# Key-value sums of a linear-attention kernel on four column strips of TensorE, and one spread on four row strips

## The chip, the core and the metric

The kernel runs on one core of one Trainium2 chip. The core has a matrix engine (TensorE, PE in the profile, with its weight loads shown apart as PEld), three engines for elementwise work (VectorE or DVE, ScalarE or ACT, GpSimd or POOL) and SyncE (SP), which here only issues DMAs. Each engine works through its own instructions in order; semaphores tie them together. TensorE reads SBUF and writes PSUM, which has eight banks of 128 partitions by 512 fp32 numbers.

The metric is the time of one execution on the device, in microseconds. The kernel before takes 426.39 us, the median of three runs (424.61 to 426.71).

## The reference

Two blocks, A and B, are applied in turn, twice, with the same weights; each is added to its input. The input has 2048 rows of 512 numbers.

```python
def _A_ref(x, wqkv, w_phi, wo):
    B, S, D = x.shape
    H = 32; Dh = D // H
    qkv = (x @ wqkv).reshape(B, S, 3, H, Dh).transpose(2, 0, 3, 1, 4)
    q, k, v = qkv[0], qkv[1], qkv[2]
    pq = jnp.einsum("bhsd,hdf->bhsf", q, w_phi)
    pk = jnp.einsum("bhsd,hdf->bhsf", k, w_phi)
    phi_q = jnp.concatenate([_softmax(pq, axis=-1), _softmax(-pq, axis=-1)], axis=-1)
    phi_k = jnp.concatenate([_softmax(pk, axis=-1), _softmax(-pk, axis=-1)], axis=-1)
    kv = jnp.einsum("bhsf,bhsd->bhfd", phi_k, v)
    z  = jnp.einsum("bhsf->bhf", phi_k)
    num = jnp.einsum("bhqf,bhfd->bhqd", phi_q, kv)
    den = jnp.einsum("bhqf,bhf->bhq", phi_q, z)[..., None] + 1e-6
    o = num / den
    return o.transpose(0, 2, 1, 3).reshape(B, S, D) @ wo

def _B_ref(x, W_gate, W_up, W_down):
    gate = jnp.einsum("bsd,df->bsf", x, W_gate)
    up = jnp.einsum("bsd,df->bsf", x, W_up)
    gate = gate * (gate > 0).astype(gate.dtype)
    return jnp.einsum("bsf,fd->bsd", gate * up, W_down)

x = x + _A_ref(_layernorm(x), A_wqkv, A_w_phi, A_wo)
x = x + _B_ref(_layernorm(x), B_W_gate, B_W_up, B_W_down)
x = x + _A_ref(_layernorm(x), A_wqkv, A_w_phi, A_wo)
x = x + _B_ref(_layernorm(x), B_W_gate, B_W_up, B_W_down)
```

Block A is linear attention with 32 heads of 16 numbers. For each head, keys and queries go through a 16 by 16 map and two softmaxes of 16 features each (one of the values, one of their negatives; called the two signs below). `kv` is then a 32 by 16 matrix for each head, summed over all 2048 rows, and `z` the sum of the key features.

## The kernel before

The 2048 rows are 16 tiles of 128 rows, and four tiles are a slab (`st` 0 to 3). The activations stay in SBUF (`x_sb`). At the start the map `w_phi` is folded into the key and query weights (`fold`, L400), so that keys come out of one product.

For each slab, `into_a` normalizes and transposes the rows and calls `keys` (L470). `keys` makes, tile by tile, the key logits and the values on PE, two exponentials on ACT (`expk`, one for each sign), the softmax sums and their reciprocals on DVE (`Zk`, `rZk`), a copy of the values on ACT (`vsb`, with a seventeenth column of ones for each head), and on POOL two products of values and reciprocals (`vhat`, one for each sign, L498). Then come the key-value sums of the slab (L501 to L515). The features are cut into eight groups `g`: two signs (`sg`) by four chunks (`c`) of 128 features, which are eight heads. For each group, four products, one for each tile, accumulate 128 features by 136 columns (eight heads by seventeen). Each is a product of every head with every head in the group; only the diagonal blocks are wanted. Three, three and two groups share a PSUM bank, and each bank is added into `kvsum` on DVE (L511, L514).

When all four slabs are summed, `sums` (L517) cuts the diagonal blocks out with `mask8`, a 128 by 8 mask that says which head a feature belongs to: eight operations write the weights `ZDw` of the denominators and eight the weights `kvbd` of the numerators.

`out_of_a` then goes slab by slab. `queries` (L533) makes the query features `expq`. `attend` (L542) multiplies them with `ZDw` on PE for the denominators (small products of 16 columns, 32 for each slab), works out on ACT and DVE one factor for each row, head and sign (`atok`), and transposes these factors into `aT`. Each factor must be spread over the sixteen features of its head. For slab 0 this is done on PE, with eight products with `EC`, a matrix of zeros and ones (L584); four of the eight results are multiplied into `expq` by DVE straight out of PSUM (L586), and four are first copied to SBUF by ACT (L590) and then multiplied (L591). `VIA` (L426) says which. For the other slabs SP writes `aT` to a scratch in HBM (L575), and eight DMAs read it back with each row sixteen times (L577). The numerators are 32 products on 32 by 32 places of the array (L600), whose outputs go to four banks. They are divided from the outset, so that a copy to `oT` and the product with `wo` follow. `glu` (L626) is block B; it has most of the products.

The order of the instructions on each engine is made by a planner (`schedule`, L119): each operation carries an estimate of how long it occupies its engine (`occ`) and when its result is there (`lat`). The planner takes the operation that can start first and breaks ties by program order. It also hands out the eight PSUM banks; an operation that needs several new banks waits until that many have been released. `plan` (L191) turns the dependences into semaphore waits. Every changed operation or estimate so changes the order of all engines.

The parts that the change touches:

Of the kernel before, what the change touches and what calls it, by code (L numbers as in the profile page):

```python
# [12 lines left out]
P = 128  # L13
# [233 lines left out]
def build_kernel(nc, A_x, A_wqkv, A_w_phi, A_wo, W_gate, W_up, W_down, out):  # L247
# [8 lines left out]
    with ExitStack() as ctx:  # L256
# [26 lines left out]
        kvsum = sb("kvsum", [8, 136], FP32)  # L283
        kvbd = sb("kvbd", [2, NC, 128])
# [16 lines left out]
        EC = sb("EC", [8, 128])  # L301
        ident = sb("ident", [128])
        mask8a = sb("mask8a", [8])
        mask8 = sb("mask8", [8])
        abT = sb("abT", [8, 512])
        scratch = [nc.dram_tensor(f"spread{i}", (64, 512), BF16, kind="Internal").ap() for i in range(2)]
# [72 lines left out]
        for i in range(NWARM):  # L379
# [8 lines left out]
        op("act", lambda e: e.activation(EC[:].rearrange("p g (h j) -> p (g h) j", j=16), ident[:, 0:64].unsqueeze(2).to_broadcast([P, 64, 16]), ACT.Copy),  # L388
           reads=[R("ident"), R("tables")], writes=[R("EC")], occ=1000, name="EC")

        op("dve", lambda e: e.tensor_tensor(BD.rearrange("p c (h f) -> p c h f", f=16),
# [34 lines left out]
        VIA = lambda c, sg: sg == 1  # L426
# [43 lines left out]
        def keys(st, b):  # L470
# [30 lines left out]
            for g0, g1 in ((0, 3), (3, 6), (6, 8)):  # L501
                ps = bank(f"kv{st}{g0}")
                for g in range(g0, g1):
                    sg, c = g // 4, g % 4
                    for j, i in enumerate(tiles):
                        mm(ps, (lambda o: lambda p: p.f32()[:, o:o + 136])((g - g0) * 136), expk[:, i, sg, c * 128:(c + 1) * 128],
                           vhat[:, i, sg, c * 8:(c + 1) * 8, :], j == 0, j == 3, [R("ek", i, sg), R("vh", i, sg)], 136, f"kv{st}")
                n = (g1 - g0) * 136
                dst = kvsum[:, g0:g1, :].rearrange("p g n -> p (g n)")
                if st == 0:  # L510
                    op("dve", (lambda ps, dst, n: lambda e: e.tensor_copy(dst, ps.f32()[:, 0:n]))(ps, dst, n),  # L511
                       reads=[ps], writes=[R("kvs", g0)], occ=490, lat=580, name="kvs")
                else:
                    op("dve", (lambda ps, dst, n: lambda e: e.tensor_tensor(dst, dst, ps.f32()[:, 0:n], ALU.add))(ps, dst, n),  # L514
                       reads=[ps, R("kvs", g0)], writes=[R("kvs", g0)], occ=490, lat=580, name="kvs")  # L515

        def sums():  # L517

            kvv = kvsum[:].rearrange("p g (h e) -> p g h e", e=17)
            for g0, g1 in ((0, 3), (3, 6), (6, 8)):  # L520
                for g in range(g0, g1):
                    sg, c = g // 4, g % 4
                    op("dve", (lambda g, sg, c: lambda e: e.scalar_tensor_tensor(ZDw[:, sg, c, 8:16], kvv[:, g, :, 16], float(EPS_DEN) if sg == 0 else 0.0,
                                                                               mask8[:], ALU.add, ALU.mult))(g, sg, c),
                       reads=[R("kvs", g0), R("mask8")], writes=[R("ZDw", sg, c)], occ=77, lat=160, name="zdw")
            for g0, g1 in ((0, 3), (3, 6), (6, 8)):
                for g in range(g0, g1):
                    sg, c = g // 4, g % 4
                    op("dve", (lambda g, sg, c: lambda e: e.tensor_tensor(kvbd[:, sg, c, :].rearrange("p (h d) -> p h d", d=16), kvv[:, g, :, 0:16],
                                                                        mask8[:].unsqueeze(2).to_broadcast([P, 8, 16]), ALU.mult))(g, sg, c),  # L530
                       reads=[R("kvs", g0), R("mask8")], writes=[R("kvbd", sg, c)], occ=201, lat=290, name="kvbd")
# [214 lines left out]
```

## Time and profile before

| | us |
|---|---|
| median of three runs | 426.39 |
| profiled execution | 424.71 |
| its span, first to last instruction | 423.0 |
| PE busy | 402.1 |
| DVE busy | 275.3 |
| ACT busy | 213.6 |
| POOL busy | 69.3 |
| key-value products (256), busy | 24.4 |
| `vhat` on POOL (64 of 1105 ns) | 68.5 |
| numerator products on 32 by 32 places (256), busy | 5.6 |
| spread products of slab 0 (16), busy | 4.2 |

The profiled execution is 1.7 us below the median. Busy time of PE is the union of matmuls that overlap: a 512-column matmul lasts 379 ns, while the next one starts 216 ns after it. The mean granted clock of PE is 0.988 of full speed; it is lower only in two stretches, around 85 to 95 and 270 to 290 us.

The run has these stages: weights and the folding (to 11.6 us), the first layer's norms, keys and key-value sums (to 69 us), attention of the first slabs of layer 0 (to 91 us), block B of layer 0 mixed with attention of later slabs and the keys of layer 1 (to 269 us), and the same for layer 1, without keys behind it (to the end).

### The profile page before, as it was taken

To read this page: it belongs to the slowest core of one execution; us is meant where nothing else is said; L and a number is where in the kernel's file an instruction comes from. 1 tells how busy PE (TensorE), PEld (TensorE's weight loads), DVE (VectorE), ACT (ScalarE), POOL (GpSimd) and SP (SyncE) were. 2 spreads that over 40 slices of the span, in tenths; PEclk is the share of its full clock that TensorE was granted. 3 is DMA by queue.
4 is the path that set the end of the run, shared out by engine and by line. 5 is a ranking of instruction groups with operands and counts; after the bars stand their busy time and mean duration, and the time that the engine had idled before them with its cause. 6 is when DMAs were issued, how large, how long until landed. Compare 5 with 4: busy or idle time off the path is not lost.

```text
span 423.0 us, 6858 instructions
## 1 busy us (share of the span) xinstructions
PE 402.1 (95%) x2684; PEld 205.1 (48%) x2731; DVE 275.3 (65%) x587; ACT 213.6 (50%) x432; POOL 69.3 (16%) x71
## 2 busy tenths in 40 slices
PE   7999999599999999999999999977999999999997
PEld 4555555354444545455455445533444544444443
DVE  4999768968479647767774446876932842664332
ACT  5999897655246522834183169855522430342320
POOL 0258780000007000620052008000000000000000
PEclk9999999989999999999999999969999999999999
DMA  8960000330000000200000000022101001301001
GB/s 265 326 210 2 2 0 7 102 107 0 2 0 2 0 2 10 97 0 2 0 2 0 2 2 2 8 99 70 39 1 50 2 0 50 108 2 37 14 0 50
DMA packets 16800, 17.66 MB, mean 42 GB/s; under 512 B 1568, under 2 KB 15744, under 8 KB 16768
## 3 DMA queue, kind: packets, MB, share of 16 engines
q1 hardware_dynamic: 15552, 16.62, 12.0%
q10 hardware_dynamic: 1216, 0.61, 0.5%
q8 instruction: 21, 0.34, 0.3%
q14 instruction: 11, 0.09, 0.1%
HBM read 14.73 MB, written 2.49 MB: 41 GB/s over the span
## 4 chain that ended last, share of the span: by engine, by line
PE 76%; ACT 15%; DVE 6%; DMA 1%; issue 1%; ACTq 0%; DVEq 0%
PE pb L323 72%; ACT expq L539 4%; ACT expk L487 3%; PE pb L327 3%; ACT ytile L449 2%; ACT vsb L495 2%; DMA hT<-in_A_wqkv_dram 1%; DVE expq L591 1%; ACT yT L463 1%; DVE stats L435 1%; PE pb L600 1%; DVE expq L586 1%; DVE Zk L489 1%; ACT Wqp L420 0%; ACT abT L590 0%
## 5 line engine op out<-in xcount | busy, mean ns | idle before, releaser
L639 ACT ACTIVATE gate_sb<-pb 128x512 bf16<-128x512 f32 (+1 forms) x88 | 52.8, 600 | 130.3 <-PE pb L323 130.2
L498 POOL TENSOR_TENSOR vhat<-vsb,rZk 128x544 bf16<-128x544 bf16 x64 | 68.5, 1105 | 193.5 <-DVE rZk L491 187.1
L641 DVE TENSOR_TENSOR hT<-gate_sb,pb 128x512 bf16<-128x512 bf16 (+1 forms) x88 | 59.6, 683 | 52.6 <-PE pb L323 52.3
L323 PE MATMUL pb<-yT,Wu 128*128 128x512 bf16 (+1 forms) x345 | 91.1, 379 | 0.2
L323 PE MATMUL pb<-yT,Wg 128*128 128x512 bf16 (+1 forms) x341 | 90.6, 379 | 0.6
L323 PE MATMUL pb<-Wd,hT 128*128 128x512 bf16 (+3 forms) x355 | 76.8, 372 | 0.4
L624 DVE TENSOR_TENSOR x_sb<-x_sb,pb 128x512 bf16<-128x512 bf16 x55 | 36.4, 685 | 48.6 <-PE pb L323 48.6
L323 PEld LDWEIGHTS pb<-Wd,hT 128*128 128x128 bf16 (+1 forms) x363 | 35.4, 98 | 40.1
L323 PEld LDWEIGHTS pb<-yT,Wu 128*128 128x128 bf16 (+1 forms) x352 | 34.9, 100 | 38.4 <-issue 0.4
L323 PEld LDWEIGHTS pb<-yT,Wg 128*128 128x128 bf16 (+1 forms) x352 | 34.4, 100 | 38.1 <-issue 1.4
L435 DVE BATCH_NORM_STATS2 stats<-x_sb 128x6 f32<-128x512 bf16 x64 | 42.4, 680 | 2.2 <-ACT x_sb L619 1.4
L489 DVE TENSOR_REDUCE Zk<-expk 128x64 f32<-128x1024 bf16 x32 | 38.4, 1204 | 7.7 <-ACT expk L487 7.5
L539 ACT ACTIVATE expq<-pb 128x512 bf16<-128x512 f32 x64 | 35.0, 696 | 12.9 <-PE pb L323 12.9
L487 ACT ACTIVATE expk<-pb 128x512 bf16<-128x512 f32 x64 | 36.3, 639 | 2.3 <-PE pb L323 0.7
L323 PE MATMUL pb<-wo_sb,oT 128*128 128x512 bf16 x121 | 31.9, 399 | 2.2 <-DVE oT L608 1.7
L323 PE MATMUL pb<-wv,yT 128*128 128x512 bf16 x124 | 33.1, 379 | 0.3
L323 PE MATMUL pb<-Wkp,yT 128*128 128x512 bf16 x124 | 32.2, 379 | 0.4 <-DVE yT L460 0.2
L323 PE MATMUL pb<-yT,Wqp 128*128 128x512 bf16 x122 | 30.9, 379 | 0.4 <-ACT Wqp L420 0.2
L463 ACT ACTIVATE yT<-pb 128x512 bf16<-128x512 bf16 x52 | 27.2, 608 | 6.3 <-PE pb L327 6.2
L610 ACT ACTIVATE oT<-pb 128x512 bf16<-128x512 f32 x28 | 15.1, 609 | 24.4 <-PE pb L600 23.6
L591 DVE TENSOR_TENSOR expq<-expq,abT 128x512 bf16<-128x512 bf16 x56 | 21.9, 424 | 8.1 <-DMA abT<-spread 8.1
L323 PE MATMUL pb<-vhat,expk 128*128 128x136 bf16 x256 | 24.4, 223 | 0.2
(68 smaller groups left out, 327.4 us busy)
## 6 DMA issues: line engine op xcount, KB each, us to landing
abT<-spread SPq DMA_DIRECT2D x48, 128.0 KB
out_dram<-x_sb SPq DMA_DIRECT2D x15, 128.0 KB, 1.7
x_sb<-in_A_x_dram SPq DMA_DIRECT2D x3, 512.0 KB, 8.8
Wg<-in_B_W_gate_dram SPq DMA_DIRECT2D x1, 1376.0 KB
Wu<-in_B_W_up_dram SPq DMA_DIRECT2D x1, 1376.0 KB
Wd<-in_B_W_down_dram SPq DMA_DIRECT2D x1, 1280.0 KB
hT<-in_A_wqkv_dram ACTq DMA_DIRECT2D x2, 256.0 KB, 5.8
wv<-in_A_wqkv_dram SPq DMA_DIRECT2D x1, 512.0 KB, 5.8
```

The costliest lines, as they stand in the source:

```text
L323: op("pe", lambda e: e.matmul(view(ps), lhsT, rhs, start=start, stop=stop), reads=reads, writes=[ps], occ=max(25.0, 0.4167 * n + 2.6), lat ...
L435: op("dve", (lambda t: lambda e: e.bn_stats(stats[:, t, :], x_sb[:, t, :]))(t), reads=[R("x", t)], writes=[R("st", t)], occ=580, lat=680, ...
L463: op("act", (lambda ps, dst: lambda e: e.activation(dst, b16half(ps).rearrange("p (c n) -> p c n", c=NC), ACT.Copy))(ps, dst), reads=[ps], ...
L487: op("act", (lambda i, s, pk: lambda e: e.activation(expk[:, i, s, :], full(pk), ACT.Exp, scale=1.0 - 2.0 * s))(i, s, pk), reads=[pk], wri ...
L489: op("dve", (lambda i, zb: lambda e: e.tensor_reduce(Zk[:, zb, :], expk[:, i, :, :].rearrange("p s (h f) -> p (s h) f", f=16), AX.X, ALU.a ...
L498: op("pool", (lambda i, s, vb, rz: lambda e: e.tensor_tensor(vhat[:, i, s, :, :], vsb[:, vb, :, :], rZk[:, rz, s * 32:(s + 1) * 32].unsque ...
L539: op("act", (lambda c, s, ps: lambda e: e.activation(expq[:, st, c, s, :], full(ps), ACT.Exp, scale=1.0 - 2.0 * s))(c, s, ps), reads=[ps], ...
L591: op("dve", (lambda c, sg, gi: lambda e: e.tensor_tensor(expq[:, st, c, sg, :], expq[:, st, c, sg, :], abT[:, gi, :], ALU.mult))(c, sg, gi ...
L610: op("act", (lambda i, pn: lambda e: e.activation(oT[:, g, i, :], full(pn), ACT.Copy))(i, pn), reads=[pn], writes=[R("oT", g, i)], occ=480 ...
L624: op("dve", lambda e: e.tensor_tensor(x_sb[:, t, :], x_sb[:, t, :], full(ps), ALU.add), reads=[R("x", t), ps], writes=[R("x", t)], occ=597 ...
L639: op("act", (lambda m, gb, pg: lambda e: e.activation(gate_sb[0:m, gb, :], pg.f32()[0:m, :], ACT.Relu))(m, gb, pg), reads=[pg], writes=[R( ...
L641: op("dve", (lambda m, gb, hb, pu: lambda e: e.tensor_tensor(hT[0:m, hb, :], gate_sb[0:m, gb, :], pu.f32()[0:m, :], ALU.mult))(m, gb, hb, pu),
```

## The change

Four things change.

First, the key-value products are made for two heads at a time. A group of 128 features is cut into four strips of 32 features (two heads), and each strip is multiplied only with the 34 columns of its own two heads. The four strips lie side by side on the array's columns (`tile_position=(0, 32 * i)`), and their results on 32 partitions each. A slab has 8 groups by 4 strips by 4 tiles, 128 products with a weight load each, where it had 32. They are two operations of the planner, one for each two tiles, each with `occ` 500. All groups together need 272 columns, so one bank holds a slab's sums, and one operation of DVE evacuates them (`occ` 350). `kvsum` shrinks from 8 by 136 to 8 by 34 columns.

Second, `sums` needs three operations of DVE in place of sixteen: the small constant is added to `z`, all of `ZDw` is written at once, and all of `kvbd` at once. `kvbd` now has 32 columns for each group. A new mask `mask2` says which of the two heads of a strip a feature belongs to.

Third, the spread of slab 0 is made by two operations of four products, each on a row strip of 32 rows (`tile_position=(32 * c, 0)`), one operation for each sign. Each takes four banks at once. `EC` shrinks from 8 to 2 groups of 128 columns and is made from a small reduction `E16` on DVE. `VIA` now takes the chunks 1 and 3 of both signs, in place of sign 1 of all chunks: four of eight, as before.

Fourth, for the row strips the rows of `aT` are laid out so that each chunk has 32 rows of which 16 are used. The write-out to the scratch has 128 rows in place of 64 (131072 bytes in place of 65536); the reads are as large as before.

```diff
@@ set-up
-        op("act", lambda e: e.activation(EC[:].rearrange("p g (h j) -> p (g h) j", j=16), ident[:, 0:64].unsqueeze(2).to_broadcast([P, 64, 16]), ACT.Copy),
-           reads=[R("ident"), R("tables")], writes=[R("EC")], occ=1000, name="EC")
+        op("dve", lambda e: e.tensor_reduce(E16[:], ident[:].rearrange("p (c r) -> p r c", r=32)[:, 0:16, :], AX.X, ALU.add),
+           reads=[R("ident")], writes=[R("E16")], occ=200, name="E16")
+        op("act", lambda e: e.activation(EC[:].rearrange("p s (h j) -> p (s h) j", j=16), E16[:].unsqueeze(2).to_broadcast([P, 16, 16]), ACT.Copy),
+           reads=[R("E16"), R("tables")], writes=[R("EC")], occ=400, name="EC")
+        op("dve", lambda e: e.tensor_reduce(mask2[:], mask8[:].rearrange("p (i h) -> p h i", h=2), AX.X, ALU.add),
+           reads=[R("mask8")], writes=[R("mask2")], occ=100, name="mask2")
...
-        VIA = lambda c, sg: sg == 1
+        VIA = lambda c, sg: c % 2 == 1
@@ keys
-            for g0, g1 in ((0, 3), (3, 6), (6, 8)):
-                ps = bank(f"kv{st}{g0}")
-                for g in range(g0, g1):
-                    sg, c = g // 4, g % 4
-                    for j, i in enumerate(tiles):
-                        mm(ps, (lambda o: lambda p: p.f32()[:, o:o + 136])((g - g0) * 136), expk[:, i, sg, c * 128:(c + 1) * 128],
-                           vhat[:, i, sg, c * 8:(c + 1) * 8, :], j == 0, j == 3, [R("ek", i, sg), R("vh", i, sg)], 136, f"kv{st}")
...
+            ps = bank(f"kv{st}")
+            def products(js):
+                def fn(e):
+                    for j in js:
+                        for g in range(8):
+                            sg, c = g // 4, g % 4
+                            for i in range(4):
+                                f0 = c * 128 + 32 * i
+                                ins = e.matmul(ps.f32()[32 * i:32 * i + 32, g * 34:g * 34 + 34], expk[:, tiles[j], sg, f0:f0 + 32],
+                                               vhat[:, tiles[j], sg, 8 * c + 2 * i:8 * c + 2 * i + 2, :], start=j == 0 and g == 0, stop=j == 3,
+                                               skip_group_check=True, tile_position=(0, 32 * i))
+                    return ins
+                return fn
+            for js in ((0, 1), (2, 3)):
+                op("pe", products(js), reads=[R("ek", tiles[j], sg) for j in js for sg in range(2)] + [R("vh", tiles[j], sg) for j in js for sg in range(2)],
+                   writes=[ps], occ=500, lat=700, name=f"kv{st}")
+            flat = kvsum[:].rearrange("p g n -> p (g n)")
+            if st == 0:
+                op("dve", lambda e: e.tensor_copy(flat, ps.f32()[:, 0:272]), reads=[ps], writes=[R("kvs")], occ=350, lat=440, name="kvs")
+            else:
+                op("dve", lambda e: e.tensor_tensor(flat, flat, ps.f32()[:, 0:272], ALU.add), reads=[ps, R("kvs")], writes=[R("kvs")], occ=350, lat=440, name="kvs")
@@ sums
+            op("dve", lambda e: e.tensor_scalar(kvv[:, 0:4, :, 16], kvv[:, 0:4, :, 16], float(EPS_DEN), None, op0=ALU.add),
+               reads=[R("kvs")], writes=[R("kvs")], occ=70, lat=160, name="eps z")
+            op("dve", lambda e: e.tensor_tensor(ZDw[:].rearrange("p s c n -> p (s c) n")[:, :, 8:16].rearrange("p g (i h) -> p g i h", h=2),
+                                                kvv[:, :, :, 16].unsqueeze(2).to_broadcast([P, 8, 4, 2]),
+                                                mask8[:].rearrange("p (i h) -> p i h", h=2).unsqueeze(1).to_broadcast([P, 8, 4, 2]), ALU.mult),
+               reads=[R("kvs"), R("mask8")], writes=[R("ZDw")], occ=140, lat=230, name="zdw")
+            op("dve", lambda e: e.tensor_tensor(kvbd[:].rearrange("p s c (h d) -> p (s c) h d", d=16), kvv[:, :, :, 0:16],
+                                                mask2[:].unsqueeze(1).unsqueeze(3).to_broadcast([P, 8, 2, 16]), ALU.mult),
+               reads=[R("kvs"), R("mask2")], writes=[R("kvbd")], occ=340, lat=430, name="kvbd")
@@ attend
-                dma("sp", lambda e: e.dma_start(scr, aT[0:64, g, :]), reads=[R("aT", g)], writes=[rs], nbytes=65536, name=f"aTo{st}")
+                dma("sp", lambda e: e.dma_start(scr, aT[:, g, :]), reads=[R("aT", g)], writes=[rs], nbytes=131072, name=f"aTo{st}")
...
-                        mm(ps, full, EC[:, gi, :], aT[:, g, :], True, True, [R("EC"), R("aT", g)], 512, f"ab{st}")
...
+        def spread(g, sg):
+            pss = [bank(f"ab0{c}{sg}") for c in range(NC)]
+            def products(e):
+                for c in range(NC):
+                    r = slice(32 * c, 32 * c + 32)
+                    ins = e.matmul(full(pss[c]), EC[r, sg, :], aT[r, g, :], start=True, stop=True, tile_position=(32 * c, 0))
+                return ins
+            op("pe", products, reads=[R("EC"), R("aT", g)], writes=pss, occ=450, lat=650, name="ab0")
+            for c in range(NC):
+                scale_by(0, c, sg, pss[c])
```

`scale_by`, which is not shown, holds the multiplications of L585 to L592, unchanged but for `VIA`.

## The prediction

> **What bounds the kernel now.** I read the page's shares and slices first, then the chain that ended last, then busy time by stretch, then the timeline around the two kinds of product that the change touches.
>
> ```profile
> PE 402.1 (95%) x2684; PEld 205.1 (48%) x2731; DVE 275.3 (65%) x587; ACT 213.6 (50%) x432; POOL 69.3 (16%) x71
> PE 76%; ACT 15%; DVE 6%; DMA 1%; issue 1%; ACTq 0%; DVEq 0%
> ```
>
> ```profile
> 11.60:49.50 37.90, 35.89 (x273) 20.05 (x275) 36.45 (x75) 37.28 (x79) 23.43 (x22) 1.00 0.45 141
> 49.50:69.00 19.50, 19.27 (x213) 12.14 (x217) 13.82 (x37) 14.81 (x30) 10.75 (x11) 1.00 0.01 2
> 69.00:91.00 22.00, 16.77 (x173) 8.90 (x173) 16.61 (x50) 16.31 (x37) 0.00 (x0) 0.92 0.22 72
> 91.00:247.00 156.00, 155.05 (x907) 77.16 (x924) 106.30 (x200) 63.79 (x124) 25.75 (x24) 1.00 0.04 12
> 247.00:269.00 22.00, 21.89 (x220) 12.84 (x222) 13.28 (x36) 20.65 (x44) 8.53 (x8) 1.00 0.01 1
> ```
>
> The columns of the second fence are stretch, length, then busy PE, weight loads, DVE, ACT, POOL, granted clock, DMA share and GB/s. From 49.5 to 69 and from 91 to 269 us TensorE has nearly no idle time and heads the chain: a microsecond of PE work there is a microsecond of the end. From 11.6 to 49.5 us the chain runs through ACT (37.28 of 37.90 busy), with DVE and PE close behind. From 69 to 91 (and, alike, 269 to 291) slab 0 of a layer passes the attention alone, and DVE and ACT set the pace. The eight key-value sums lie at 20, 35, 46, 58 us (layer 0) and 133, 176, 219, 258 us (layer 1): five or six of eight where PE is the bound.
>
> The rows that price the change:
>
> ```profile
> 137.84 0.93 PE L323 MATMUL pb<-vhat,expk 128*128 128x136 bf16 x13
> 65.76 2.42 PE L323 MATMUL pb<-ZDw,expq 128*128 128x16 bf16 x90
> 119.54 1.68 PE L323 MATMUL pb<-Wd,hT 128*128 128x512 bf16 x7
> 121.14 0.65 PE L600 MATMUL pb<-expq,kvbd 32*32 32x512 bf16 x32
> 121.73 0.82 PE L323 MATMUL pb<-yT,Wg 128*128 128x512 bf16 x3
> ...
> 84.90 0.20 PEld L600 LDWEIGHTS pb<-expq,kvbd 32*32 32x32 bf16 x32 [2.45 <-DVE expq L591]
> 76.50 0.33 PEld L600 LDWEIGHTS pb<-expq,kvbd 32*32 32x32 bf16 x32
> 76.64 0.19 PEld L600 LDWEIGHTS pb<-expq,kvbd 32*32 32x32 bf16 x4
> ```
>
> The second number is the group's time from first start to last end. The reader is to see four prices. A 136-column product takes (0.93 - 0.22)/12 = 59 ns from start to start (0.22 is one matmul's own duration). A 16-column product on the whole array takes (2.42 - 0.17)/89 = 25 ns. Products on separate 32x32 places start far closer: after a wait of 2.45 us all 32 weight loads start within 0.20 - 0.09 = 0.11 us, 3.5 ns apart. But at 76.50, right behind a quick run of 18 small products, the same 32 loads need 0.33, and the last four (the third row, cut out of the second) start (0.19 - 0.09)/3 = 34 ns apart. I read this as supply: up to about 32 load-and-matmul pairs stand ready in front of PE, and when they are used up a new pair comes every 34 ns.
>
> **The change, part by part.**
>
> *Key-value sums on PE.* Removed: 32 products of 136 columns per slab, 16 per two tiles: 16 x 59 ns = 0.95 us. Added: 64 products of 34 columns with a weight load each per two tiles, as one operation. The trace has no such product. From below: 64 x 3.5 ns = 0.22 us (places never used twice in a row). From above: 64 x 34 ns = 2.18 us (nothing ready, all supplied). I take 32 pairs ready, because PE comes from 512-column products (216 ns for each pair, so supply runs ahead), and 32 supplied: 32 x 34 = 1.09 us, if a strip itself can go on every 4 x 17 = 68 ns, which the 25 ns of the small products leaves room for. Then the change of the array's division: the last 512-column product before the L600 group starts at 119.54 + 1.68 - 0.38 = 120.84, L600 at 121.14, 0.30 later where 0.22 is usual; behind it the last start is 121.14 + 0.65 - 0.37 = 121.42 and the next matmul 121.73, 0.31 later. So some 0.09 us at each end, 0.18 per operation. Sum per two tiles: 1.09 + 0.18 - 0.95 = +0.32 us; bounds -0.55 and +1.41. Sixteen such: +5.1 us, bounds -8.8 and +22.6.
>
> How much counts: the twelve operations of slabs 2 to 7 in full, 3.8 us; the four of slabs 0 and 1 lie where ACT heads the chain and PE has 2 us idle in 37.9: none to all of 1.3 us, half taken, 0.6. Together +4.4.
>
> The operation also waits for both tiles' vhat on POOL (1.1 us for each half tile) where single products slipped in before. Behind it on PE stand the gate and up products or the queries, and behind those ACT's gate and DVE's h, which idle 130 and 53 us over the run. It cannot start before the last vhat, but neither could the last 10 of the old ones. I take 0; a stall of one vhat, 1.1 us, in a slab or two is the upper end.
>
> The Trainium skill bears on this price: "TensorEngine Tiling (Array Packing)", Instruction Overhead, says that a matmul pays some 60 cycles however few columns it has, and warns against taking the tiling factor from a dimension that is already small. The Trainium skill, "TensorE: Matmul & The Clock Gate", Back-to-back issue gap, puts those 60 cycles at about 25 ns for up to 64 columns; by it an operation would be an estimated 64 x 25 ns = 1.6 us instead of 1.09. The trace agrees for the whole array (25 ns) and not for separate places (3.5 ns).
>
> *DVE.* Three evacuations per slab, 0.58 + 0.58 + 0.43 us, become one of 272 columns, 0.43 (its row is there already): -1.15 us, eight times. The sums before each layer, 8 x 0.163 + 8 x 0.291 = 3.6 us, become three operations: 0.16 for the bias, 0.16 to 0.29 for 64 elements (0.23 taken), 0.43 for 256 elements by the 272-column row; 0.8 in all. DVE loses 15 us of work, of which I credit nothing: in the PE-bound stretches it idles anyway, and between 21 and 32 us, where DVE is full, ACT is as full and heads the chain. If DVE were the one there, -1.15 us. From the last vhat (63.32) to the first long run of denominators (65.76) the old way took 2.4 us; the new takes 0.2 to start, 1.09, 0.22 for the last matmul, 0.43, 0.16, 0.23: 2.3. No difference, and queries fill PE meanwhile.
>
> *Spread of slab 0.* Eight 512-column products (8 x 216 ns = 1.7 us) become two operations of four side by side, 2 x (0.22 + 0.18) = 0.8 us. PE idles there; DVE is busy without a break from 71.3 to 76.2 us with the same eight multiplications as before. Worth 0; if the second operation must wait for four free banks at once, DVE may lose one multiplication of 0.68 us in each layer; if DVE gets its first operands sooner, -0.3. Behind the spread on PE stand slab 1's denominators.
>
> *DMAs.* The write-out doubles to 128 KB for the three later slabs, on SP, with eight reads of 128 KB and then nothing urgent behind it. The 64 KB took 2.0 us to land, the 128 KB output writes 1.7: 0 to +0.3 us, hidden where PE is the bound; slab 1's multiplications are held by DVE's own queue (they follow each other with norms between), so 0.
>
> *Set-up.* EC on ACT shrinks from 1.06 us; two small reductions on DVE come in, by the mask copies' 0.23 us each. All end before 7.75 us, when PE gets its weights from the DMA: 0.
>
> **Sum:** +4.4 us. The profiled execution took 424.71 us (span 423.0), 1.7 below the median of 426.39; so 429.1 on its own scale, 430.8 on the median's, which I forecast as 431.
>
> **Rivals.**
>
> *A, the strips run free, faster.* If the pairs are supplied as fast as the strips take them, an operation costs 0.22 + 0.18 = 0.40 us, 0.55 less than before; with seven eighths on the path, -7.7 us: 418.7 for it in full. It decides at a pace of (0.95 - 0.18)/64 = 12 ns per pair: below, the change gains. For it: the 0.20 us burst. Against: no burst in the trace is longer than 32 pairs, and the 34 ns of the last four.
>
> *B, every small product costs its 25 ns.* If four strips that share all the rows follow each other like products on the whole array, an operation is 64 x 25 = 1.6 + 0.18 us, +0.83: 16 x 0.83 x 7/8 = +11.6, 438. For it: the denominators' row, and that in L600 a place comes round only after sixteen pairs, here after four. Against: the 3.5 ns between places. This is also the skill's rule from above, told here as this kernel would show it.
>
> *C, hidden.* The order of all engines is planned anew, with PE charged 0.5 us per operation, and one bank less for most of a slab. If DVE's 1.15 us in the prologue, the slabs 0 and 1, and gaps at the change of slabs give back 3 us or more of the 4.4: 425 to 428.
>
> **Chances.** Forecast 0.57 (own range 428.6 to 435, to a stall or two of POOL above and a half-hidden prologue below), A 0.18, B 0.16, C 0.09. A measurement of this kernel tells about 0.5%, 2.1 us, from no change. So faster 0.18, same 0.09, slower 0.73. The range 420 to 441 leaves out the strongest half of A and the cases beyond B, some 0.15.
>
> **What would show it.** Right: groups of 64 pairs of 1.1 to 1.3 us on PE with the first 30 or so loads a few ns apart and the rest 34; a gap of 0.3 us behind the 512-column product before; PE's chain longer in 91 to 247; DVE busy near 260 us with the span not shorter. Wrong: all 64 within 0.4 us (A), or even steps of 25 ns (B). The forecast falls too if the set-aside DVE time turns out to have been on the path, or if the new order leaves PE waiting for POOL.

## The result, and the profile after

| | before | after |
|---|---|---|
| median, us (11 runs each) | 425.75 | 423.05 |
| lowest to highest | 424.23 to 428.67 | 420.68 to 424.99 |
| profiled execution | 424.71 | 420.98 |
| its span | 423.0 | 419.2 |
| mean granted clock of PE in it | 0.988 | 0.974 |

The ratio is 0.9927, 95% interval 0.9898 to 0.9956: the changed kernel is 0.7% faster, 2.7 us by the medians. The forecast was 431, slower; the time lies in the range given, on the other side of no change.

The first part of the page and its chain of engines, after:

```profile
PE 397.9 (95%) x3499; PEld 195.7 (47%) x3499; DVE 265.0 (63%) x547; ACT 212.0 (51%) x432; POOL 69.2 (17%) x71
PE 87%; DVE 8%; ACT 2%; DMA 1%; POOL 1%; issue 0%; ACTq 0%; DVEq 0%
```

PE has some 800 more matmuls and is busy 4.2 us less; most of ACT's 15% of the chain has gone to PE. The same stretches as in the prediction (stretch, length, busy PE, weight loads, DVE, ACT, POOL, clock, DMA share, GB/s):

```profile
11.60:49.50 37.90, 36.17 (x534) 19.65 (x533) 34.69 (x71) 37.46 (x78) 25.72 (x24) 1.00 0.44 141
49.50:69.00 19.50, 18.59 (x384) 10.78 (x382) 10.91 (x23) 18.69 (x41) 8.56 (x8) 1.00 0.01 3
69.00:91.00 22.00, 15.65 (x144) 6.72 (x141) 18.10 (x51) 11.66 (x26) 0.00 (x0) 0.77 0.34 115
91.00:247.00 156.00, 156.00 (x1221) 75.02 (x1220) 103.37 (x194) 66.35 (x132) 25.57 (x24) 1.00 0.02 8
247.00:269.00 22.00, 21.56 (x318) 11.84 (x317) 10.42 (x21) 20.38 (x45) 8.52 (x8) 1.00 0.01 2
```

From 91 to 247 us PE is the bound without a gap. From 69 to 91 the granted clock fell from 0.92 to 0.77: something new is there.

The strip products on the timeline of after (start, length of the group from first start to last end). The fourth row is cut out of the first:

```profile
133.44 0.57 PEld L516 LDWEIGHTS pb<-vhat,expk 128*32 128x32 bf16 x64 [0.42 <-issue]
133.44 0.66 PE L516 MATMUL pb<-vhat,expk 128*32 128x34 bf16 x64
137.81 0.66 PE L516 MATMUL pb<-vhat,expk 128*32 128x34 bf16 x64
133.66 0.34 PEld L516 LDWEIGHTS pb<-vhat,expk 128*32 128x32 bf16 x31
```

An operation takes 0.66 us. Its first 33 pairs start within 133.66 - 133.44 = 0.22 us (by the single records 3 to 4 ns from strip to strip and some 15 ns before the first strip comes round again, 25 ns for each four), and the last 31 follow (0.34 - 0.09)/30 = 8.3 ns apart. The prediction had 34 there.

By single records, the 512-column product before the operation starts 0.309 us ahead of it where 0.216 is usual, first to last start take 0.478, and the next matmul starts 0.118 later: 0.309 + 0.478 + 0.118 - 0.216 = 0.69 us of PE for an operation. The 16 products of before took 16 x 59 ns = 0.944. So each operation gains 0.255 us, and 16 of them 4.1.

Where the time went, by the start of the first key exponential and of the last key-value product of some slabs (us; layers and slabs are counted from 0):

| | before | after | difference of the stage |
|---|---|---|---|
| first key exponential on ACT (no key-value product yet) | 12.96 | 11.82 | -1.1 |
| layer 0, slab 3 (end of the prologue) | 64.3 | 62.6 | -0.5 |
| layer 1, slab 0 (behind the attention of slab 0) | 139.4 | 138.3 | +0.6 |
| layer 1, slab 1 | 182.8 | 181.0 | -0.7 |
| layer 1, slab 2 | 226.0 | 223.7 | -0.5 |
| layer 1, slab 3 | 265.1 | 262.3 | -0.5 |
| end | 423.0 | 419.2 | -1.0 |

The three slabs in the PE-bound stretch gain 0.5 to 0.7 us each, 1.7 in all: two operations of 0.255 a slab.

The first 1.1 us are not the change's. They are there before any key-value product, and two executions of the same start-up differ as much. PE's rows of before, and of the kernel before with unused products that come only behind 60 us (the last experiment below), then the first exponentials of before and after:

```profile
8.58 1.06 PE L327 MATMUL pb<-ident,ytile 128*128 128x128 bf16 x8
8.52 0.61 PE L327 MATMUL pb<-ident,ytile 128*128 128x128 bf16 x8
12.96 0.60 ACT L487 ACTIVATE expk<-pb 128x512 bf16<-128x512 f32 x1 [0.48 <-PE pb L323]
11.82 1.09 ACT L493 ACTIVATE expk<-pb 128x512 bf16<-128x512 f32 x2 [0.48 <-PE pb L325]
```

The same eight transposes are 107 ns apart in the one and 55 in the other, and PE's weights land at 7.75 and 8.06 us; from there to the first exponential it is 5.2 and 4.1 us. In the profiled execution of after it is 4.0. Without this difference the two spans are 2.6 us apart, close to the 2.7 of the medians. So the prologue itself gains 0.5, and the way into the attention of layer 0 loses. The mark between them is not quite like for like: behind it some 17 products of queries are left before and 7 after, 10 x 0.216 = 2.2 us of PE.

That loss, in windows of after around the spread of slab 0:

```profile
64.00:67.00 3.00, 3.00 (x106) 2.80 (x103) 0.93 (x4) 2.42 (x7) 0.00 (x0) 1.00 0.02 5
67.00:70.50 3.50, 2.00 (x40) 1.25 (x37) 3.11 (x13) 2.71 (x9) 0.00 (x0) 0.94 0.00 0
70.50:74.00 3.50, 0.61 (x4) 0.11 (x4) 3.50 (x9) 2.20 (x6) 0.00 (x0) 0.50 0.17 56
74.00:80.00 6.00, 5.10 (x45) 1.86 (x46) 4.82 (x16) 2.19 (x5) 0.00 (x0) 0.50 0.54 181
```

The queries are done at 64 us, so only 16-column products and transposes are left for PE (2.00 of 3.50 us busy), then two short spread operations. The granted clock is halved from some 70 to 80 us. PE's own rows of after show what that costs:

```profile
70.79 0.61 PE L645 MATMUL pb<-aT,EC 32*128 32x512 bf16 x4 [0.70 <-DVE zm L569]
74.63 1.08 PE L604 MATMUL pb<-expq,kvbd 32*32 32x512 bf16 x32 [3.23 <-DVE expq L635]
76.52 1.89 PE L325 MATMUL pb<-wo_sb,oT 128*128 128x512 bf16 x4 [0.27 <-ACT oT L614]
```

The numerators take 1.08 us where the same 32 took 0.65 in the prediction's row, and the four 512-column products of `wo` 1.89 us: by their starts 427 ns each, against 216 at full clock. Before, the clock was halved only from 85.5 to 89 us (0.51 there) and in layer 1.

### The profile page after: what moved, and what is told of

The parts are those of the page before. It is cut to its first block, busy times and chain, and to the rows that moved or that the text cites. A ratio compares the mean times of both kernels' runs of the same rounds, so it can differ in the third digit from the quotient of the medians.

```text
span 419.2 us, 8409 instructions
## 1 busy us (share of the span) xinstructions
PE 397.9 (95%) x3499; PEld 195.7 (47%) x3499; DVE 265.0 (63%) x547; ACT 212.0 (51%) x432; POOL 69.2 (17%) x71
## 4 chain that ended last, share of the span: by engine, by line
PE 87%; DVE 8%; ACT 2%; DMA 1%; POOL 1%; issue 0%; ACTq 0%; DVEq 0%
PE pb L325 80%; PE pb L329 4%; PE pb L516 2%; DVE stats L441 2%; DMA hT<-in_A_wqkv_dram 1%; DVE expq L635 1%; DVE expq L630 1%; DVE Zk L495 1%; DVE atok L575 1%; PE pb L604 1%; POOL vhat L504 1%; ACT expk L493 0%; DVE rZk L497 0%; DVE zm L569 0%; DVE ytile L458 0%; ACT expq L550 0%
## 5 line engine op out<-in xcount | busy, mean ns | idle before, releaser
L325 PE MATMUL pb<-yT,Wg 128*128 128x512 bf16 (+1 forms) x352 | 92.9, 379 | 0.0
L325 PE MATMUL pb<-Wd,hT 128*128 128x512 bf16 (+2 forms) x363 | 77.4, 372 | 0.0
L325 PE MATMUL pb<-wo_sb,oT 128*128 128x512 bf16 x128 | 35.0, 410 | 0.6 <-ACT oT L614 0.6
L325 PE MATMUL pb<-Wkp,yT 128*128 128x512 bf16 x128 | 33.2, 379 | 0.0
L329 PE MATMUL pb<-ident,ytile 128*128 128x128 bf16 x256 | 22.5, 224 | 2.2 <-DVE ytile L458 1.9
L329 PEld LDWEIGHTS pb<-ident,ytile 128*128 128x128 bf16 x256 | 17.8, 100 | 10.5 <-DVE ytile L458 3.0
```

The source lines that it names most:

```text
L325: op("pe", lambda e: e.matmul(view(ps), lhsT, rhs, start=start, stop=stop), reads=reads, writes=[ps], occ=max(25.0, 0.4167 * n + 2.6), lat ...
L329: op("pe", lambda e: e.transpose(view(ps), src, ident[:]), reads=list(reads) + [R("ident")], writes=[ps], occ=56, lat=220, name=name)
```

## The experiments

Medians in microseconds; "before" is the kernel before, run on the same chip in the same series. The ratio is to it. A kernel's runs spread by some 2 us to either side of the median.

| | median | before | ratio | 95% |
|---|---|---|---|---|
| strips without the new spread | 423.35 | 426.01 | 0.9939 | 0.9904 to 0.9973 |
| new spread alone | 426.95 | 426.01 | 1.0022 | 0.9995 to 1.0049 |
| VectorE's work put back, behind the sums too | 431.47 | 426.01 | 1.0135 | 1.0083 to 1.0188 |
| late unused products | 423.47 | 426.01 | 0.9941 | 0.9912 to 0.9971 |
| twice the pairs | 438.9 | 426.35 | 1.0309 | 1.0267 to 1.035 |
| one operation a slab | 426.76 | 426.35 | 1.0026 | 1.0001 to 1.0051 |
| four operations a slab | 423.26 | 426.35 | 0.9934 | 0.9908 to 0.996 |
| early unused products | 421.1 | 425.55 | 0.9894 | 0.9868 to 0.992 |
| the same, without the new spread | 420.35 | 425.55 | 0.9871 | 0.9847 to 0.9894 |
| planner told the true length | 422.44 | 425.55 | 0.9924 | 0.9893 to 0.9954 |
| VectorE's evacuations padded | 424.72 | 425.55 | 0.9971 | 0.9947 to 0.9995 |
| before, with early unused products | 424.65 | 426.54 | 0.9963 | 0.9935 to 0.999 |

### The two halves of the change

The first kernel keeps the strips and `sums` of the change and has the spread, `EC`, `VIA` and the scratch of before; the second the other way round.

```diff
-            if st == 0:
-                for sg in range(2):
-                    spread(g, sg)
-            ...
+            for c in range(NC):
+                for sg in range(2):
+                    ...
+                        mm(ps, full, EC[:, gi, :], aT[:, g, :], True, True, [R("EC"), R("aT", g)], 512, f"ab{st}")
```

> The changed kernel with the spread of slab 0 as it was before (eight products on the whole array, EC of 8 groups, 64 rows of factors); the key-value strips, the one bank and the three-operation sums stay. Theory T1 (PE time): a strip operation costs PE 0.69 us where sixteen products cost 0.95, 16 x 0.26 = 4.1 us, and the new spread costs something, because PE stands still longer in slab 0 and its granted clock halves from 70 to 80 us: this kernel 421 to 422 us, 1 to 2 below the changed one (423). Rival T2 (the spread helps too): 424 or more, above the changed one.

> The kernel before with nothing but the new spread (row strips, EC of 2 groups, 128 rows of factors). T1: 426 to 428 us, no faster than before (425.8) or up to 2 slower, with a halved clock of some 10 us in slab 0 of layer 0, as in the changed kernel. T2: 423 to 424.5, the spread brings its part.

Strips alone 423.35 us, as fast as the whole change (0.9939 against 0.9927); the new spread alone makes no difference that can be told (1.0022, the interval holds 1). So by the medians all of the gain belongs to the key-value part, and the theory that had the new spread cost something beside the strips was too optimistic for the strips alone.

The clock is another matter. The strips without the new spread, from 69 to 91 us:

```profile
69.00:91.00 22.00, 15.70 (x169) 8.39 (x172) 18.00 (x50) 13.56 (x30) 0.00 (x0) 0.92 0.28 92
```

That is the 0.92 of before, where the whole change has 0.77. Over their executions the mean clock is 0.976 to 0.984 for the strips alone and 0.967 to 0.976 for the whole change. So the longer halved stretch comes with the new spread, not with the strips, although it does not show in the medians.

### What the pace of the pairs hangs on

Each product of the strips is made an operation of its own. The work is the same; each now increments a semaphore and may be placed on its own.

```diff
-            def products(js):
-                ...
-            for js in ((0, 1), (2, 3)):
-                op("pe", products(js), ...)
+            for j in range(4):
+                for g in range(8):
+                    ...
+                        op("pe", ..., reads=[R("ek", tiles[j], sg), R("vh", tiles[j], sg)], writes=[ps], occ=8, lat=200, name=f"kv{st}")
```

> The changed kernel with every strip product as an operation of its own, each with its own semaphore increment, as all of PE's other products have. A look at the pace alone. If increments set the pace: 25 to 34 ns from start to start within a strip run. If not: 3 to 8 ns as in the changed kernel. The time itself: over 430 us if the pace is 25 ns or more (1024 x 17 ns more).

It took 430.85 us, a single execution. Its timeline at the first slab; the second row is cut out of the first:

```profile
21.52 0.82 PEld L514 LDWEIGHTS pb<-vhat,expk 128*32 128x32 bf16 x48 [0.42 <-ACT expk L493]
21.84 0.50 PEld L514 LDWEIGHTS pb<-vhat,expk 128*32 128x32 bf16 x13
```

The first 33 pairs go as before, 3 to 16 ns apart by the single records; then it is (0.50 - 0.09)/12 = 34 ns a pair. That is the prediction's number to the nanosecond, in the prediction's place, and here it is the pace of strip pairs that each increment a semaphore. Without increments the same pairs came every 8.3 ns. Increments alone do not make 34 ns: in the prediction's row of `ZDw`, 90 products on the whole array, each with a weight load and an increment, follow each other at 25 ns. Why strips with increments are slower than those is open. In the trace of before, the four L600 loads 34 ns apart stood behind 18 small products, each with its own increment; that these had used up the supply fits, but only the pair of kernels, with and without increments, is shown.

The Trainium skill, "TensorE: Matmul & The Clock Gate", Part 3: Packing small matmuls, says both that products on different tiles of the array start about 4 ns apart and that increments by every product are serialized at about 26 ns each. The first agrees here (3 to 4 ns); the second points the right way, and here it was 34.

The second kernel gives every operation 64 more pairs of 28 columns, whose results nobody reads.

```diff
+                    for j in js:
+                        for g in range(8):
+                            ...
+                                ins = e.matmul(ps.f32()[32 * i:32 * i + 32, 272 + g * 28:272 + g * 28 + 28], ...)
```

> The changed kernel with twice as many load-and-matmul pairs in every strip operation: 64 more, of 28 columns, into the unused columns of the same bank, results unused. In the changed kernel's trace the second half of an operation goes at 8.3 ns per pair. If that is the supply, 64 more pairs cost 64 x 8.3 = 0.53 us, 16 operations 8.5 us, and with seven eighths on the path 7.5 us: 430 to 431 us. If the first reading of 34 ns held for longer runs than 64 pairs: 64 x 34 = 2.2 us each, over 450. If PE's time in these operations is not what sets the end: 424 or less.

The time is 438.9 us, 12.5 above before and 16 above the changed kernel. First to last start took 1.01 us where nothing disturbed it (0.478 in the changed kernel): 64 pairs more for 0.53 us, 8.3 ns each, so the pace does not wear off. Apart from stalls the steady slabs grew by 1.07 us each, two operations of 0.53, as expected. The rest was not foreseen: 430 to 431 had been expected. The added half of one operation, by PE's rows:

```profile
50.68 0.66 PE L516 MATMUL pb<-vhat,expk 128*32 128x34 bf16 x64
51.16 0.53 PE L524 MATMUL pb<-vhat,expk 128*32 128x28 bf16 x42
53.50 0.32 PE L524 MATMUL pb<-vhat,expk 128*32 128x28 bf16 x22 [1.81 <-issue]
```

Amid an operation, with nothing to wait for, PE stood for some 2 us. There are five such stalls (1.55, 1.99, 0.69, 0.54 and 0.29 us), and one of 1.97 us right behind an operation, at 272 us. Four of the five lie in the prologue, which ended 9.2 us later than in the changed kernel: 1.4 of it was there at the first key exponential, 4.5 are these stalls, and up to 8 x 0.53 the pairs. The queue that the page calls instruction had 35 packets, against 27 in the changed kernel and 21 before. That PE ran out of instructions is argued from this, not shown. The length of an operation is not the reason: the next kernel has as many pairs in one, 27 packets and no such stall.

### The size of an operation

One operation of 128 pairs a slab, as shown, then four of 32 (`occ` 250):

```diff
-            for js in ((0, 1), (2, 3)):
+            for js in ((0, 1, 2, 3),):
...
-                   writes=[ps], occ=500, lat=700, name=f"kv{st}")
+                   writes=[ps], occ=1000, lat=1200, name=f"kv{st}")
```

> The changed kernel with one strip operation of 128 pairs for each slab in place of two of 64. Saved: one change of the array's division in and out per slab, 0.18 us, 8 x 0.18 = 1.4 us of PE, less 0.5 us at each change into attention, because no pair can start before the last tile: 421.5 to 422.5 us by T1 (PE time). 423 or more if the division's changes cost nothing in the end.

> The changed kernel with four strip operations of 32 pairs per slab, one for each tile. By T1 two more changes of the array's division for each slab, 16 x 0.18 = 2.9 us of PE, less what is saved because 32 pairs never run out of ready ones (32 x 6.3 ns in place of 8.3): 425 to 426 us. 423 or less if waiting for the second tile, not the division, is what costs.

One operation: 426.76, all of the gain gone, where 421.5 to 422.5 had been expected. The steady slabs were 0.1 to 0.2 us shorter still, but the prologue ended 3.7 us later than in the changed kernel. Its timeline there:

```profile
60.95 4.28 POOL L504 TENSOR_TENSOR vhat<-vsb,rZk 128x544 bf16<-128x544 bf16 x4
65.37 1.19 PE L516 MATMUL pb<-vhat,expk 128*32 128x34 bf16 x128 [1.55 <-POOL vhat L504]
66.65 0.44 DVE L529 TENSOR_TENSOR kvsum<-kvsum,pb 128x272 f32<-128x272 f32 x1 [5.91 <-PE pb L516]
67.70 0.65 PE L325 MATMUL pb<-ZDw,expq 128*128 128x16 bf16 x19 [1.14 <-DVE ZDw L536]
```

All key-value work of the slab waits for POOL's last `vhat`, PE has run out of queries, and everything behind waits for the sums. This is the stall that the prediction had as the upper end for operations of two tiles. It needs a whole slab in one operation to appear.

Four operations: 423.26, no different from two. Each took 0.40 us, and a tile's 32 pairs all run at the quick pace; four cost some 0.2 us a slab more than two. The steady slabs were 0.3 us longer, and other stages gave it back; 425 to 426 had been expected.

The planner charges 500 ns for what takes 690. Told the truth, it orders PE, ACT and DVE otherwise from the first slab's sums on:

```diff
-                   writes=[ps], occ=500, lat=700, name=f"kv{st}")
+                   writes=[ps], occ=690, lat=850, name=f"kv{st}")
```

> The changed kernel with the planner told 690 ns for a strip operation, as the trace has it, in place of 500; no instruction is added or removed, only their order may change. PE time theory: 423 within 1 us. If the order of the instructions is worth as much as the change itself: 2 us or more away from 423, on either side.

422.44 us, within 1 us of the changed kernel. Its prologue ended 1.4 us earlier (61.2), and the way to the sums of layer 1 gave that back (138.9 against 138.3): the order alone moves the mark between the two stages by more than the change's 0.5 us.

### VectorE's saved work

The first kernel adds operations of 408 columns (0.577 us) whose results nobody reads: two behind each evacuation and six behind the sums of a layer. The second, which is shown, has the two behind the evacuations of slabs 0 to 2 alone, so it gives back there just what the change took away (0.58 + 0.58 + 0.43 against 0.43).

```diff
+            for k in range(2 if st < 3 else 0):
+                op("dve", ...(padout[:, 0:408], padin[:, 0:408], padin[:, 104:512], ALU.add)..., reads=[R("padin"), R("kvs")], writes=[R("padout", st)], occ=490, lat=580, name="pad")
```

> The changed kernel with DVE work put back that computes nothing: two sums of 408 fp32 numbers behind each evacuation of key-value sums (some 1.0 us) and six in each layer's sums (some 2.9 us), about 14 us of DVE in all, as much as the change took away. T1: DVE's relief is off the path except at the change into attention, 423 to 425 us. Rival T3 (the relief of DVE is the gain): 426 us or more, the whole gain is lost.

> The changed kernel with two DVE sums of 408 fp32 numbers (1.15 us, what the change took from each evacuation) put back behind the evacuations of slabs 0 to 2 of each layer, none at the change into attention. PE time theory: the steady part has the same times from slab to slab, 423 to 424 us. Rival (DVE's relief is the gain everywhere): 425 us or more.

All pads: 431.47. The prologue ended at 64.4 us, 1.8 later than in the changed kernel, the way into attention grew by 6.5, the steady slabs by nothing, the change in layer 1 by 2.2. The six pads behind the sums lie ahead of the first softmax factors, where the old operations for `kvbd` were hidden, so this end overshoots. The second kernel avoids that: 424.72 us, between the two expectations; the prologue ends at 64.5, and the steady slabs are as in the changed kernel. Its windows over the prologue, from 32 us to its end, and those of the kernel before and the changed one:

```profile
32.00:64.50 32.50, 31.07 (x528) 16.12 (x532) 24.86 (x37) 32.15 (x65) 26.14 (x24) 1.00 0.01 2
```

```profile
32.00:64.30 32.30, 31.87 (x238) 18.42 (x241) 25.66 (x44) 30.15 (x59) 25.61 (x24) 1.00 0.00 1
```

```profile
32.00:62.60 30.60, 30.60 (x528) 15.79 (x527) 22.22 (x33) 30.60 (x62) 25.14 (x24) 1.00 0.01 2
```

With VectorE's 1.15 us a slab put back, the prologue of the changed kernel ends 1.9 us later (64.5 against 62.6), although the strips are as quick; without it PE and ACT have no gap at all from 32 us on. Hardly any of the 1.9 is won back: at the first sums of layer 1 it is still 1.7 us late (140.0 against 138.3). So VectorE's work counts in this prologue. That the gain on the kernel before is VectorE's does not follow. Of the 1.6 us, 1.1 came ahead of the first exponential, and with the pads the order is another, with one product of queries left behind the mark where some 17 were left before. In the PE-bound slabs VectorE's work is worth nothing, as the prediction had it.

### The halved clock

The first kernel lets PE work during the multiplications of slabs 0 and 1: two unused products of 512 columns behind each of seven. The second adds such products from the start of the change into attention on, in both layers; the third is the second without the new spread. The diff is the second's.

```diff
+        def keep(st, trigger, n, last=False):
+            ...
+                for _ in range(n):
+                    ins = e.matmul(full(kb), ident[:], wo_sb[:, 0, :], start=True, stop=True)
...
+            if st == 0:
+                keep(st, [R("zden", g)], 2)
```

> The changed kernel with two products of 512 columns, results unused, behind each of the first seven multiplications of slabs 0 and 1 in each layer, where PE stands still. T1: the granted clock stays up from 70 to 90 and from 270 to 290 us, the output products of slab 0 take 216 ns in place of 427, 2 us saved in each layer: 419 to 421 us. Rival: the clock is not what sets slab 0's time there (DVE is): 423, or 424 where the extra products delay the numerators.

> The changed kernel with unused 512-column products from the start of each change into attention: two behind the denominators, the reciprocal, the factors and their transposes of slab 0, one behind each of its first seven multiplications, two behind those of slab 1. In the earlier trial the granted clock had halved at 70 us, before the first extra product at 73. If the halved clock is what the change loses in slab 0: clock 0.99 or more, 420.5 to 421.5 us. Rival: DVE's chain of multiplications sets that stretch, and the clock only fills idle time: 423 to 424 us at a higher clock.

> The same early products in the kernel with the strips but the spread as before. Clock theory: 420 to 421 us, the fastest so far. Rival (DVE's chain): 423 to 424 us.

The late products brought nothing (423.47): the clock had halved at some 70 us, the first of them came at 73.3, and 13 of them took 4.65 us at half clock and held the numerators back to 77.9 us. The early ones kept it, as the windows of the second kernel show:

```profile
67.00:70.50 3.50, 3.18 (x44) 1.71 (x43) 3.26 (x14) 2.17 (x8) 0.00 (x0) 1.00 0.02 5
70.50:74.00 3.50, 2.02 (x14) 0.59 (x14) 3.47 (x10) 2.97 (x8) 0.00 (x0) 1.00 0.19 65
74.00:80.00 6.00, 5.60 (x60) 2.54 (x61) 6.00 (x18) 2.28 (x4) 0.00 (x0) 1.00 0.53 181
```

It takes 421.1 us, and the third 420.35 (0.9871), the fastest of all, beyond both kernels. More work for PE made the run shorter: for the strips without the new spread the two intervals lie apart, for the whole change (0.9894 against 0.9927) they overlap. PE's rows of the second and then of the third, which answer to those of the changed kernel:

```profile
74.88 0.65 PE L626 MATMUL pb<-expq,kvbd 32*32 32x512 bf16 x32
74.32 0.65 PE L633 MATMUL pb<-expq,kvbd 32*32 32x512 bf16 x32
77.04 0.81 PE L324 MATMUL pb<-wo_sb,oT 128*128 128x512 bf16 x3
```

The numerators take 0.65 us again, and three products of `wo` 0.81, 216 ns apart. But the strips without the new spread had this pace here without unused products too. By the profiled executions the third kernel is 0.2 us behind them at the last key-value product (262.1 against 262.0) and 0.8 ahead at the end (418.4 against 419.2): what can be located lies in layer 1, and it is less than the 3 us of the medians.

The Trainium skill, "TensorE: Matmul & The Clock Gate", Part 1, has the clock halved after an idle window of about 3.4 us. Here it was halved behind 3.5 us in which PE was busy for 2.00 with small products and transposes, before the long idle time began: to be half busy was not enough, by this run.

The last kernel gives the same early products to the kernel before.

> This is the kernel before with the same early unused products (512 columns, results read by nothing, at the start of the change into attention of both layers) that brought the kernel with strips alone from 423.35 to 420.35 us. Theory K, the clock costs every version alike: the kernel before gains as much, to 423 to 424 us, ratio to the kernel before 0.992 to 0.996, and with the clock held the strips are worth 3 to 4 us, which is what 16 operations of 0.69 instead of 0.944 us sum to (4.1 us). Theory L, only the strips' earlier end of the prologue leaves the engine sparse: the kernel before, which runs its change into attention at a granted clock of 0.94 already, gains nothing or loses the time of the extra products, 425 to 427 us, and with the clock held the strips are worth 5 us or more, that is the 4.1 us of the operations and the 1.5 to 2 us of VectorE's relief in the prologue beside it.

424.65 us, ratio 0.9963, the mean clock of the profiled run 1.000: the kernel before gains too, 1.6 us by the ratio (0.4 to 2.8 by its interval). That is nearer to theory K, a little short of the gain that it named. Of the profiled executions, this one gains 0.8 us behind the last key-value product, and none in layer 0 behind the prologue. With the clock held in both, the strips are worth 0.9871/0.9963 = 0.991, 3.9 us (with both intervals, 2.3 to 5.5), against 2.6 without the products. By these values the early products bring the strips (0.9871 against 0.9939, 2.9 us) more than the kernel before, but within the intervals the two may be alike. That the held clock is what brings it is likely and not shown: the kernels with early products were planned anew, too.

## Why the prediction was wrong

The forecast was +4.4 us on the profiled run's scale; it became -3.8 there, -2.7 by the medians.

**The key-value sums on PE: the step that failed.** "When they are used up a new pair comes every 34 ns" was read off four loads of a kernel in which the products ahead increment semaphores, and carried over to an operation in which only the last does. The first 32 pairs were ready, as said, and took 0.22 us, which the sum left out; the 32 supplied cost 8.3 ns each. The term of 1.09 us measured 0.478 from first to last start, both halves together, and +0.32 us an operation became -0.255. Rival A had the right side and the right point of decision (12 ns a pair; 0.478/63 = 7.6 ns measured), but took 3.5 ns for every pair, 0.40 us an operation where it is 0.69. Rival B, even steps of 25 ns, holds for one strip and not for four: each strip comes round after 25 ns in the quick half, with the three others in between. So the 60 cycles of the Trainium skill's "TensorEngine Tiling (Array Packing)", Instruction Overhead, do not add up across strips here.

**The change of the array's division** was sized right: 0.18 us forecast; 0.309 - 0.216 = 0.093 us ahead of an operation and 0.118 from its last start to the next matmul, which holds that last product's own slot.

**How much of it counts.** Twelve operations in full was too many to show. The six of layer 1's last three slabs showed their 0.255 each and a little more (0.5 to 0.7 us a slab, 1.7 in all). Those of layer 1's first slab stand in a stage that lost 0.6, and the eight of layer 0 in one that gained 0.5: there the operations' gain cannot be told from the new order.

**VectorE credited with nothing** is doubtful for the prologue. The prediction named the 1.15 us between 21 and 32 us as a bound and took 0, because ACT headed the chain there. Put back, 3 x 1.15 us cost the changed kernel 1.9 there; how much the relief gave against the kernel before, and which of ACT's steps had waited for VectorE, stays open. In the PE-bound stretches 0 was right.

**The wait for both tiles' `vhat`** was rightly taken at 0 for two tiles, and the one-operation kernel shows the stall that was kept as the upper end.

**The spread of slab 0** was worth 0 by the medians, as forecast. **The write-out** of 128 KB took 3.0 us to land, beyond the bound of 2.0 + 0.3. Its size alone does not set this: 64 KB took 2.6 us in the strips without the new spread, and 128 KB took 1.8 in the changed kernel with early products. DMA stayed at 1% of the chain.

**The clock** was in the view (0.92 from 69 to 91 us) and in no term. With the new spread PE was sparse behind the queries and the clock was halved from some 70 us on; with the old spread the strips kept the 0.92 of before. What that cost is not shown: the whole change and the strips alone have nearly the same ratio (0.9927 and 0.9939).

The sum by the runs, on the profiled scale: the start -1.1, which is not the change's, the rest of the prologue -0.5, from there to the first sums of layer 1 +0.6 (+1.1 without the 0.5 of that slab's two operations), the three slabs behind them -1.7, the rest -1.0, together -3.7 of the -3.8. The last -1.0 lies behind the last key-value product and was not taken apart. That 16 x 0.255 = 4.1 us is near the whole -3.8 is luck.

## What to carry to other kernels

A pace read off a trace belongs to its kind of instructions: look whether the products signal a semaphore one by one before carrying it to an operation in which only the last does. Work on an engine that "idles anyway" is priced by padding it back, stage by stage: 3.5 us put back cost 1.9 in the prologue and as much in the steady slabs cost nothing. Two profiled executions are compared from an early mark that the change does not touch: here 1.1 of 3.8 us lay ahead of it. Whoever shortens TensorE's work ahead of a thin stretch should look at the granted clock in it: a few unused products at its start may be worth more than they cost.

## What the runs showed of the hardware

- Pairs of weight load and matmul on four column strips: some 33 at 25 ns for each four, then 8.3 ns a pair without semaphore increments and 34 ns with one each; up to 128 pairs the 8.3 ns held. On the whole array, 90 pairs with an increment each came every 25 ns.
- From products on the whole array to strips and back cost 0.093 us ahead and up to 0.118 behind; operations of 32, 64 and 128 pairs took 0.40, 0.69 and 1.22 us of PE.
- The granted clock was halved after 3.5 us at which PE was 57% busy (2.00 of 3.50) with 16-column products and transposes; busy for 3.18 of 3.50, it stayed at 1.00. Unused products that held it made the kernel before 1.6 us faster and the strips without the new spread 2.9, by the medians.
- The same eight transposes at 8.5 us were 107 ns apart in one execution and 55 in another, and the first key exponential came 5.2 or 4.1 us behind the weights.
- With twice the pairs (2048 in 16 operations), PE stood up to 2 us in the midst of an operation, with nothing to wait for; with 1024 pairs in 8 operations of 128 it did not. Why is open.
